# First pair's keys and queries through hardware queues, second batch's loads ahead of the weights, last store in halves

## The chip, the cores and the metric

The kernel runs on one core of a Trainium2 chip. The metric is device time in microseconds (us), the median of several executions. The profile is one execution recorded by the hardware profiler; its span is about 1.8 to 2.1 us shorter than the measured time of the same execution. A run is called slow when it is over 1.5% above the fastest run of the same kernel; such runs are left out of every ratio here.

## The reference

Attention over 8 batches, 12 heads, 448 positions and 64 columns a head, with one added to the softmax's denominator, is followed by a feed-forward layer (768 to 2048 to 768) whose activation is a rational function. Inputs and outputs are float32.

```python
def _attn_ref(q, k, v):
    scores = np.matmul(q, k.transpose(0, 1, 3, 2)) / np.sqrt(q.shape[-1])
    m = np.max(scores, axis=-1, keepdims=True)
    e = np.exp(scores - m)
    return np.matmul(e / (np.sum(e, axis=-1, keepdims=True) + np.exp(-m) + 1e-09), v)
# x = attention output as (B*S, H*D)
# h = x @ w_in                              GEMM1
# g = (a0 + a1 h + a2 h^2 + a3 h^3) / (1 + |b0| |h| + |b1| h^2 + 1e-6)
# out = g @ w_out                           GEMM2
```

## The kernel before

Everything is computed in f16 with f32 accumulation. GpSimd issues all loads but those of two small constants (`abc`, `bbc`), and its loads cast f32 to f16 on the way. Batches 0 and 1 are transposed by TensorE (`tq`, `tk`: nine or eight 112-column blocks of queries, four of keys, for each pair of heads), later batches by the DMA. For a pair of heads come score tiles (`sps`), exponentials on ScalarE (`e`), sums (`den`) and products (`u`) with the values, the scaled result (`xt`) on VectorE, and then GEMM1 (`hp`), the rational function and GEMM2 (`op`).

```python
def load_qk(b, qd, which):              # 4 heads a load, from GpSimd, with the cast
    ...
    nc.gpsimd.dma_start(out=loaded[b, which][...], in_=by_quad(src, b, qd))

def transpose_q(b, p):                  # one pair of heads
    tq = ps.tile([128, 9 * T], F16, tag="gen", bufs=4, name="tq")
    for i, g in enumerate(range(g0, g1)):
        nc.tensor.transpose(tq[:, i * T:(i + 1) * T],
                            loaded[b, "q"][:, g * D:(g + 2) * D], ident[0:T, 0:T])
    # turn(): VectorE copies tq to qT
...
load_qk(0, 0, "k")
load_qk(0, 0, "q")
...
abc = const.tile([128, 4], F32)         # the constants a, on every partition
nc.sync.dma_start(out=abc, in_=moe_a.unsqueeze(0).to_broadcast([128, 4]))
bbc = ...                               # the constants b, likewise; VectorE makes |b| of them
...
def weights(b, h, i):
    e = att.tile([T, 2, S], F16, tag="e", name="e", bufs=12)
    nc.scalar.activation(out=e, in_=sps[0:T, :, 0:S], func=AF.Exp, scale=scale)
...
def outputs(b, tl, nh, eng):
    copied(eng, osb[:, nh * HD:(nh + 1) * HD], ops.pop((b, tl, nh))[:, 0:HD])
    if nh == 1:                         # both halves of the row copied: store them
        ...
        store(b - 1, SM, SR, osb[0:SR])
        store(b, SM, SR, osb[SR:128])
```

The order on TensorE, ScalarE, VectorE and GpSimd is fixed when the kernel is built, by a small planner. Each unit of work has a stream, a key, an estimated duration, the units that it depends on, and the buffers that it takes; the planner takes the unit that can start soonest, then the one with the lowest key. GEMM1 of batch 0 cannot start before all 12 heads of batch 0 are through, so up to there TensorE has only scores, sums, products and transposes. The order of the first loads was

```python
first_loads(("k0", 0), ("q0", 0), ("q0", 1), ("k0", 1), ("v0", 0), ("q0", 2), ("k0", 2),
            ("v0", 1), ("v0", 2), ("q1", 0), ("k1", 0), ("q1", 1), ("w", 0), ("w", 1),
            ("k1", 1), ("w", 2), ("w", 3), ("q1", 2), ("k1", 2), ("v1", 0), ...)
```

The softmax here doesn't subtract the row's maximum and nothing guards it: scores larger than these inputs give would overflow.

Of the kernel before, what the change touches and what calls it, by code (L numbers as in the profile page):

```python
# [16 lines left out]
class Plan:  # L17
# [29 lines left out]
    def order(self, switch, reluctance):  # L47
        at = dict.fromkeys(self.streams, 0)
        mode = None
        while at:  # L50
            ahead = defaultdict(list)
            for s, i in at.items():
                name, key, cost, fn, deps, takes, m = self.streams[s][i]
                r = self.ready(deps, takes)
                if r is None:
                    continue
                for eng in cost:
                    t = max(self.free[eng], r)
                    k = key
                    if eng == "PE" and m != mode:  # L60
                        k += reluctance
                    ahead[eng].append((t, k, s))
            first = None
            for eng, some in ahead.items():
                soon = min(t for t, _, _ in some)
                k, t, s = min((k, t, s) for t, k, s in some if t <= soon + 1e-9)
                if first is None or t < first[0]:
                    first = t, eng, s
# [19 lines left out]
def kernel(  # L88
# [30 lines left out]
    nc.scalar.preload_act_table_set("natural_log_exp_and_others")  # L119
# [12 lines left out]

    loaded = {}
    NB = H * NJ // 2

    def load_qk(b, qd, which):
        w = NJ * D
        if qd == 0:
            if which == "q":
                q4 = ld.tile([T, D + H * NJ * D + D], F16, tag="q4", name="q4")  # L140
                eng = nc.vector if b == 0 else nc.gpsimd
                eng.memset(q4[:, 0:D], 0.0)
                eng.memset(q4[:, D + H * NJ * D:], 0.0)
                loaded[b, "q"] = q4
            else:
                loaded[b, "k"] = ld.tile([T, H * NJ * D], F16, tag="k4", name="k4")
        src, o = (q, D) if which == "q" else (k, 0)
        nc.gpsimd.dma_start(
            out=loaded[b, which][:, o + 4 * qd * w:o + 4 * (qd + 1) * w].rearrange(
                "p (h x) -> p h x", x=w),  # L150
            in_=by_quad(src, b, qd))
# [60 lines left out]
    load_qk(0, 0, "k")  # L212
    load_qk(0, 0, "q")
# [34 lines left out]

    def load_w_out(i):
        if i == 0:  # L250
            nc.gpsimd.tensor_copy(out=gate[0:1, 0:1], in_=loaded[2, "qT"][0:1, 2 * NB * T:2 * NB * T + 1])
# [3 lines left out]

    xts = {}
    ets = {}


    sps_of = {}  # L260

    def scores(b, h, i):
        qT, kT = loaded[b, "qT"], loaded[b, "kT"]
        sps = ps.tile([128, 2, 512], F32, tag="sps", bufs=2, name="sps")
        for half in range(2):
            r = slice(64 * half, 64 * half + 64)
            c = (4 * h + 1 - half) * T
            nc.tensor.matmul(  # L268
                out=sps[0:T, half, 0:S],
                lhsT=kT[r, (2 * h + i) * T:(2 * h + i + 1) * T],  # L270
                rhs=qT[r, c:c + S], start=True, stop=True,
            )
# [8 lines left out]
    def by_heads(dst, b, qd, w):  # L281
        for j in range(NJ):
            for t in range(4):
                nc.tensor.matmul(  # L284
                    out=dst[32 * t:32 * t + 32, 0:S], lhsT=w(4 * qd + t, j),
                    rhs=ets[b, 4 * qd + t, j // 2][:, j % 2, :],
# [7 lines left out]
    def sums(b, qd):  # L294
        dens[b, qd] = ps.tile([128, 512], F32, tag="gen", bufs=4, name="den")
        by_heads(dens[b, qd], b, qd, lambda h, j: ones)

    def sums_ln(b, qd):
        rdens[b, qd] = att.tile([128, S], F32, tag="rden", name="rden")
        nc.scalar.activation(out=rdens[b, qd], in_=dens.pop((b, qd))[:, 0:S],  # L300
                             func=AF.Ln, bias=one_c)

    def sums_inv(b, qd):
        nc.scalar.activation(out=rdens[b, qd], in_=rdens[b, qd], func=AF.Exp, scale=-1.0)

    def products(b, qd, half):
        v4 = loaded[b, "v"]
        u = us[b, qd, half] = ps.tile([128, 512], F32, tag="gen", bufs=4, name="u")
        by_heads(u, b, qd, lambda h, j: v4[:, h, j, 32 * half:32 * half + 32])

    def attended(b, qd, half):
        if (qd, half) == (0, 0):
            xts[b] = xp.tile([128, NDC, S], F16, tag="xt", name="xt")
        nc.vector.tensor_tensor(  # L314
            out=xts[b][:, 2 * qd + half, :], in0=us.pop((b, qd, half))[:, 0:S],
            in1=rdens[b, qd], op=ALU.mult
        )
# [3 lines left out]
    def gemm1(b, fc):  # L321
        xt = xts[b]
        hp = ps.tile([128, 512], F32, tag="gen", bufs=4, name="hp")
        for c in range(NDC):
            nc.tensor.matmul(  # L325
                out=hp[:, 0:S], lhsT=w_in_sb[:, c, fc * 128:(fc + 1) * 128],
                rhs=xt[:, c, :], start=(c == 0), stop=(c == NDC - 1),
            )
        hps[b, fc] = hp
        if fc % FG == 0:  # L330
            gs[b, fc // FG] = gp.tile([128, FG, S], F16, tag="g", name="g")
# [3 lines left out]
    def copied(eng, out, src):  # L335
        if eng == "ACT":
            nc.scalar.activation(out=out, in_=src, func=AF.Copy)
        else:
            nc.vector.tensor_copy(out=out, in_=src)  # L339

    def hidden(b, fc, eng):
        copied(eng, gs[b, fc // FG][:, fc % FG, :], hps.pop((b, fc))[:, 0:S])
# [8 lines left out]
    def temp(tag, f0, n):  # L351
        return moe.tile([128, FG, S], F16, tag=tag, name=tag)[:, f0:f0 + n, :]

    def rational(b, gi, f0, n, step):
        h = gs[b, gi][:, f0:f0 + n, :]
        at = b, gi, f0
        if step == 0:
            m = ns[at] = temp("w", f0, n)
            nc.vector.tensor_scalar(out=m.bitcast(U16), in0=h.bitcast(U16),
                                    scalar1=0x7FFF, scalar2=None, op0=ALU.bitwise_and)  # L360
        elif step == 1:
            c = cs[at] = temp("c", f0, n)
# [31 lines left out]
    def store(b, c0, n, src):  # L394
        dst = out[b * S:(b + 1) * S, :].rearrange("(p j) d -> j p d", j=NJ)
        r = 0
        while r < n:
            j, p0 = divmod(c0 + r, T)
            m = min(T - p0, n - r)
            nc.sync.dma_start(out=dst[j, p0:p0 + m], in_=src[r:r + m, :])  # L400
# [19 lines left out]
    def outputs(b, tl, nh, eng):  # L420
        if nh == 0:
            osbs[b, tl] = moe.tile([128, DM], F32, tag="osb", name="osb")
        osb = osbs[b, tl]
        copied(eng, osb[:, nh * HD:(nh + 1) * HD], ops.pop((b, tl, nh))[:, 0:HD])
        if nh == 1:
            if tl < NW:
                store(b, tl * 128, 128, osb)
            else:
                store(b - 1, SM, SR, osb[0:SR])
                store(b, SM, SR, osb[SR:128])  # L430
# [4 lines left out]
        free=dict(DMA=3.7, PE=3.0, ACT=3.0, DVE=4.0),  # L435
# [4 lines left out]
    def load_step(stream, key, b, qd, which):  # L440
        takes = [(which + "4", (which, b))] if qd == 0 else []
        fn = (lambda: load_v(b, qd)) if which == "v" else (lambda: load_qk(b, qd, which))
        if (b, qd) == (0, 0) and which != "v":
            fn = None
        add(stream, ("ld", which, b, qd), key, {"DMA": (1.2, 4.4)}, fn, takes=takes)
# [11 lines left out]
    def first_loads(*steps):  # L457
        for what, i in steps:
            if what == "w":
                w_in_step(i)  # L460
            else:
                load_step("ld", 0, int(what[1]), i, what[0])

    first_loads(("k0", 0), ("q0", 0), ("q0", 1), ("k0", 1), ("v0", 0), ("q0", 2), ("k0", 2),
                ("v0", 1), ("v0", 2), ("q1", 0), ("k1", 0), ("q1", 1), ("w", 0), ("w", 1),
                ("k1", 1), ("w", 2), ("w", 3), ("q1", 2), ("k1", 2),
                ("v1", 0), ("v1", 1), ("v1", 2))
    for b in range(2, B):
# [6 lines left out]
        if b == 2:  # L475
            for i in range(NWO):
                add("ld", ("w_out", i), 0, {"DMA": (15.7 / NWO, 15.7 / NWO + 3)},
                    lambda i=i: load_w_out(i), deps=[("xb", 2, 2)])

    EV = -100  # L480
    for b in range(B):
        for p in range(NP):
            n = b * NP + p
            if b < 2:
                for which, fn, busy, copy in (("q", transpose_q, 0.7, (0.55, 0.7)),
                                              ("k", transpose_k, 0.3, (0.3, 0.45))):
                    first = [(which + "T", (which + "T", b)) for which in "qk"]
                    add("tp", ("tp", b, p, which), n - 0.6, {"PE": (busy, busy + 0.1)},
                        lambda b=b, p=p, fn=fn: fn(b, p),
                        deps=[("ld", which, b, p // 2)] + (  # L490
                            [("ld", which, b, (p + 1) // 2)]
                            if which == "q" and p < NP - 1 else []),
# [6 lines left out]
            for h in (2 * p, 2 * p + 1):  # L499
                at = n + 0.5 * (h % 2)  # L500
                if b < 2:
                    turned_by = [("tc", b, p, "q"), ("tc", b, p, "k")]
                else:
                    turned_by = [("xb", b, i) for i in range(3)]
                for i in range(2):
                    add("s", ("s", b, h, i), at, {"PE": (0.23, 0.33)},
                        lambda b=b, h=h, i=i: scores(b, h, i), deps=turned_by,
                        takes=[("sps", ("sps", b, h, i))],
                        uses=[("qT", b), ("kT", b)], mode="rows")
                    add("ex", ("ex", b, h, i), at, {"ACT": (0.797, 0.95)},  # L510
                        lambda b=b, h=h, i=i: weights(b, h, i), deps=[("s", b, h, i)],
                        takes=[("e", ("e", b, h, i))], uses=[("sps", b, h, i)])
        for qd in part:
            n = b * NP + 2 * qd
            es = [(b, h, i) for h in range(4 * qd, 4 * qd + 4) for i in range(2)]
            add("av", ("den", b, qd), n + 2.02, {"PE": (0.76, 0.86)},
                lambda b=b, qd=qd: sums(b, qd), deps=[("ex",) + x for x in es],
# [119 lines left out]
```

## Time and profile before

| | before |
|---|---|
| median of 4 runs | 441.56 us (440.56 to 441.81) |
| span of the profiled run (441.07 us) | 439.3 us |
| first transpose | 7.09 us |
| first exponential | 10.18 us |
| first GEMM1 matmul | 38.78 us |
| last matmul ends | 434.19 us |

The page's busy times and the granted clock in 40 slices of 11 us (tenths of full speed). PE stands for TensorE's matmuls, PEld for its weight loads, DVE for VectorE, ACT for ScalarE, POOL for GpSimd, SP for SyncE:

```profile
PE 422.8 (96%) x3346; PEld 214.6 (49%) x3346; DVE 361.9 (82%) x536; ACT 309.0 (70%) x331; POOL 88.3 (20%) x145
...
PEclk9998999999999999999999999999999999999999
```

TensorE is nearly always occupied, but that does not say that it works at full rate. Counting matmuls by kind and pricing each at the shortest duration that the timeline shows for it (GEMM1 unit 1.14 us, GEMM2 unit 2.6, pair of score matmuls 0.23, a unit of sums or products 0.76) gives an estimate of 400.6 us for all of them. The rest is lost mainly at the start. The timeline of TensorE, ScalarE and VectorE there (start us, duration us, engine, line, operation, out<-in, count, and in brackets the idle time before and what ended it):

```profile
7.09 1.00 PE L196 MATMUL tq<-ident,q 112*128 112x112 f16 x9 [7.09 <-DMA q<-in_q_dram]
...
9.51 0.99 PE L268 MATMUL sps<-qT,kT 64*112 64x448 f16 x4
...
10.18 1.72 ACT L278 ACTIVATE e<-sps 112x896 f16<-112x896 f32 x2 [8.16 <-PE sps L268]
...
12.34 2.53 ACT L278 ACTIVATE e<-sps 112x896 f16<-112x896 f32 x3 [0.44 <-PE sps L268]
```

Only 12 us into the run do exponentials follow one another without gaps. The chain that ended last, at the end of the first batch's attention (start us, us, what), and two windows of 1 us in the same stretch (busy us and number of instructions of each engine, granted clock, DMA share, GB/s):

```profile
28.64 4.96 ACT e L278 x6
...
33.65 0.62 PE sps L268 x2
34.27 1.61 PE den L284 x13
35.88 2.05 PE u L284 x25
...
38.94 1.14 PE hp L325 x6
```

```profile
core 0: us, PE busy (x) PEld busy (x) DVE busy (x) ACT busy (x) POOL busy (x), PEclk, DMA share, GB/s
32.00:33.00 1.00, 0.56 (x4) 0.25 (x4) 0.00 (x0) 1.00 (x2) 0.69 (x2) 1.00 1.23 203
34.00:35.00 1.00, 1.00 (x14) 0.39 (x16) 0.00 (x0) 1.00 (x2) 0.60 (x1) 0.50 1.27 198
```

ScalarE's exponentials lead the chain. TensorE does little beside them from 29 us on (0.40 to 0.56 of each microsecond up to 33), the clock falls to half at 33.4 us, and the sums and products of the last four heads take 3.7 us in place of 2.4. The Trainium skill ("TensorE: Matmul & The Clock Gate", "What's actually happening") says that the array's clock is halved after an idle window of about 3.4 us and released after a busy one of that length. This trace agrees in the half rate and in the length: by its clock record (part of the trace, no view of the profile) 0.50 was granted for 3.41 us from 33.42.

### The profile page before, as it was taken

Reading aid. Unit: us, or ns where it says so; the run is one execution under the profiler, and the core shown is the slowest. Engines: PE = TensorE matmul, PEld = TensorE weight load, DVE = VectorE, ACT = ScalarE, POOL = GpSimd, SP = SyncE. Lnnn points to the kernel's source line nnn. Section 1 sums busy time; section 2 is a strip of 40 time slices with the busy share of each in tenths; the row PEclk is TensorE's granted clock in tenths of the full one; section 3 lists DMA queues with packets and bytes.
Section 4 is the critical chain, followed back from the end, with each engine's and each line's share of the span. In section 5 each row is a group of like instructions: output and inputs, shape, how many; then the busy total and the mean of one; then the engine's idle time right before and its main releaser. Section 6 shows DMA issues by size and latency. Waiting matters only on the chain.

```text
span 439.3 us, 8052 instructions
## 1 busy us (share of the span) xinstructions
PE 422.8 (96%) x3346; PEld 214.6 (49%) x3346; DVE 361.9 (82%) x536; ACT 309.0 (70%) x331; POOL 88.3 (20%) x145
## 2 busy tenths in 40 slices
PE   3979999999999999999999999999999999999995
PEld 2534544445444544545445445454544455556663
DVE  2533899999999988799899988799979768999821
ACT  1997998897898785677887856868699674674400
POOL 8466025503241005020050001020000000004100
PEclk9998999999999999999999999999999999999999
DMA  9999989999899169911798049410011011102222
GB/s 123 199 203 197 183 144 184 203 183 198 179 156 181 38 127 154 172 36 38 139 185 131 1 98 170 95 36 17 23 36 36 3 37 36 39 0 73 72 73 72
DMA packets 93476, 46.90 MB, mean 107 GB/s; under 512 B 52480, under 2 KB 89856, under 8 KB 93440
## 3 DMA queue, kind: packets, MB, share of 16 engines
q0 software_dynamic: 38848, 22.81, 38.2%
q1 hardware_dynamic: 54592, 23.58, 27.4%
q8 instruction: 26, 0.43, 0.4%
q14 instruction: 10, 0.08, 0.1%
HBM read 45.62 MB, written 11.01 MB: 129 GB/s over the span
## 4 chain that ended last, share of the span: by engine, by line
PE 83%; DVE 8%; ACT 6%; issue 1%; DMA 1%; POOL 0%; POOLq 0%
PE op L412 34%; PE hp L325 28%; PE sps L268 9%; PE u L284 7%; PE den L284 4%; ACT e L278 4%; DVE g L339 2%; DVE w L372 1%; DMA q<-in_q_dram 1%; DVE w L374 1%; ACT c L379 1%; ACT c L381 1%; DVE g L377 1%; PE tq L196 1%; DVE xt L314 1%
## 5 line engine op out<-in xcount | busy, mean ns | idle before, releaser
L278 ACT ACTIVATE e<-sps 112x896 f16<-112x896 f32 x192 | 165.9, 914 | 57.6 <-PE sps L268 57.0
L325 PE MATMUL hp<-xt,w_in_sb 128*128 128x448 f16 x768 | 158.0, 353 | 0.0
L412 PE MATMUL op<-w_out_sb,g 128*128 128x384 f16 x768 | 131.1, 327 | 0.0
L325 PEld LDWEIGHTS <-w_in_sb 128*128 128x128 f16 x768 | 70.2, 98 | 76.4 <-issue 17.3
L412 PEld LDWEIGHTS <-g 128*128 128x128 f16 x768 | 73.5, 98 | 53.8 <-issue 5.4
L379 ACT ACTIVATE c<-c,oneeps_c 128x1792 f16<-128x1792 f16 (+1 forms) x33 | 57.4, 1743 | 29.9 <-DVE c L367 29.9
L339 DVE CAST g<-hp 128x448 f16<-128x448 f32 x109 | 66.8, 617 | 13.3 <-PE hp L325 13.3
L372 DVE TENSOR_TENSOR w<-w,g 128x1792 f16<-128x1792 f16 (+1 forms) x66 | 70.0, 1061 | 0.7
L391 POOL COPY gx<-g 128x256 f16<-128x256 f16 x32 | 19.9, 641 | 237.9 <-DVE g L377 136.1
L268 PE MATMUL sps<-qT,kT 64*112 64x448 f16 x384 | 61.9, 380 | 4.3 <-ACT e L278 3.9
L381 ACT ACTIVATE c<-c 128x1792 f16<-128x1792 f16 (+1 forms) x33 | 54.2, 1647 | 0.3
L314 DVE TENSOR_TENSOR xt<-u,rden 128x448 f16<-128x448 f32 x48 | 27.8, 616 | 21.6 <-PE sps L268 8.1
L339 DVE COPY osb<-op 128x384 f32<-128x384 f32 x51 | 28.2, 553 | 20.6 <-PE op L412 20.6
L374 DVE TENSOR_SCALAR w<-w,abc 128x1792 f16<-128x1792 f16 (+1 forms) x66 | 44.3, 672 | 0.6
L284 PE MATMUL u<-e,v 112*32 112x448 f16 x768 | 41.1, 356 | 0.0
L268 PEld LDWEIGHTS <-kT 64*112 64x112 f16 x384 | 20.1, 126 | 41.6 <-issue 40.2
L377 DVE TENSOR_TENSOR g<-w,c 128x1792 f16<-128x1792 f16 (+1 forms) x33 | 35.0, 1061 | 1.0
L367 DVE TENSOR_TENSOR c<-c,w 128x1792 f16<-128x1792 f16 (+1 forms) x33 | 35.0, 1062 | 0.8
L156 POOL DMA_DIRECT2D v<-in_v_dram x24 | 17.7, 740 | 70.0 <-PE u L284 67.8
L284 PEld LDWEIGHTS <-v 112*32 112x32 f16 x768 | 20.8, 98 | 16.4 <-issue 1.0
L369 DVE TENSOR_SCALAR w<-g,abc 128x1792 f16<-128x1792 f16 (+1 forms) x33 | 24.2, 733 | 0.6
L363 DVE TENSOR_SCALAR c<-w,babs 128x1792 f16<-128x1792 f16 (+1 forms) x33 | 24.3, 738 | 0.3
(36 smaller groups left out, 217.7 us busy)
## 6 DMA issues: line engine op xcount, KB each, us to landing
k<-in_k_dram POOLq DMA_DIRECT2D x24, 224.0 KB, 9.9
q<-in_q_dram POOLq DMA_DIRECT2D x24, 224.0 KB, 9.3
v<-in_v_dram POOLq DMA_DIRECT2D x24, 224.0 KB, 8.6
w_in_sb<-in_moe_w_in_dram POOLq DMA_DIRECT2D x16, 192.0 KB, 7.9
w_out_sb<-in_moe_w_out_dram POOLq DMA_DIRECT2D x4, 768.0 KB, 11.7
out_dram<-osb SPq DMA_DIRECT2D x8, 336.0 KB, 2.7
out_dram<-osb SPq DMA_DIRECT2D x8, 288.0 KB, 3.0
out_dram<-osb SPq DMA_DIRECT2D x8, 240.0 KB, 2.6
```

The source lines that it names most:

```text
L268: nc.tensor.matmul(out=sps[0:T, half, 0:S], lhsT=kT[r, (2 * h + i) * T:(2 * h + i + 1) * T], rhs=qT[r, c:c + S], start=True, stop=True,)
L278: nc.scalar.activation(out=e, in_=sps[0:T, :, 0:S], func=AF.Exp, scale=scale)
L284: nc.tensor.matmul(out=dst[32 * t:32 * t + 32, 0:S], lhsT=w(4 * qd + t, j), rhs=ets[b, 4 * qd + t, j // 2][:, j % 2, :], start=(j == 0), s ...
L325: nc.tensor.matmul(out=hp[:, 0:S], lhsT=w_in_sb[:, c, fc * 128:(fc + 1) * 128], rhs=xt[:, c, :], start=(c == 0), stop=(c == NDC - 1),)
L339: nc.vector.tensor_copy(out=out, in_=src)
L367: nc.vector.tensor_tensor(out=c, in0=c, in1=m, op=ALU.mult)
L372: nc.vector.tensor_tensor(out=m, in0=m, in1=h, op=ALU.mult)
L374: nc.vector.tensor_scalar(out=m, in0=m, scalar1=a1 if step == 5 else a0, scalar2=None, op0=ALU.add)
L377: nc.vector.tensor_tensor(out=h, in0=m, in1=c, op=ALU.mult)
L379: nc.scalar.activation(out=c, in_=c, func=AF.Ln, bias=oneeps_c)
L381: nc.scalar.activation(out=c, in_=c, func=AF.Exp, scale=-1.0)
L412: nc.tensor.matmul(out=op[:, 0:HD], lhsT=lhs(fc), rhs=w_out_sb[:, fc, nh * HD:(nh + 1) * HD], start=(fc == 0), stop=(fc == NFC - 1),)
```

## The change

The intent is to start the first exponential sooner, to have more work for TensorE before the first GEMM1, and to shorten the end. The first two key heads and three query heads are loaded as f32 through the hardware queues of ScalarE and SyncE and narrowed by VectorE and ScalarE, because, as the Trainium skill says ("DMA: Bandwidth & Descriptors", "SWDGE vs HWDGE vs iDMA"), a cast during the load is possible from GpSimd only. Loads that GpSimd issues are called software loads below. The second batch's keys and queries are loaded ahead of the first weight. The last output tile is stored in halves by two queues. The planner got new keys, and until 35 us of its own reckoning it changes between kinds of matmul without reluctance.

```diff
+    early = {"k": 2, "q": 3}
+    def load_early(which):
+        ...
+        wide[which] = moe.tile([128, DM], F32, tag="osb", name="osb")
+        eng = nc.sync if which == "q" else nc.scalar
+        eng.dma_start(out=wide[which][0:T, 0:n * w]..., in_=by_quad(...)[:, 0:n])
+    def narrow(which, eng):             # k on VectorE, q on ScalarE
+        copied(eng, loaded[0, which][:, o:o + n], wide[which][0:T, 0:n])
-    load_qk(0, 0, "k")
-    load_qk(0, 0, "q")
+    load_early("k")
+    nc.scalar.preload_act_table_set("natural_log_exp_and_others")
+    load_early("q")
+    load_qk(0, 0, "k", early["k"])      # the heads that are left, as before
+    load_qk(0, 0, "q", early["q"])
 ...
-    first_loads(("k0", 0), ("q0", 0), ("q0", 1), ("k0", 1), ("v0", 0), ("q0", 2), ("k0", 2),
-                ("v0", 1), ("v0", 2), ("q1", 0), ("k1", 0), ("q1", 1), ("w", 0), ("w", 1), ...
+    first_loads(k0.0, q0.0, q0.1, q0.2, k0.1, v0.0, k0.2, v0.1, k1.0, q1.0, k1.1, k1.2,
+                q1.1, q1.2, v0.2, w.0, w.1, w.2, v1.0, k2.0, v1.1, w.3, ...)   # shortened
 ...
+        if (b, tl, nh) == (B - 1, NW, 1):
+            for half, to in enumerate((nc.sync, nc.scalar)):
+                r = slice(64 * half, 64 * half + 64)
+                copied(("DVE", "ACT")[half], osb[r, HD:], ops[b, tl, nh][r, 0:HD])
+                store(b - 1 + half, SM, SR, osb[r], HD, DM, to)
 ...  (new keys S_AT, G1_AT, G2_AT, R_AT, LN_AT; patience and calm in the planner;
 ...   branches for split query halves and for reciprocals on VectorE, never taken)
```

The counts of matmuls (3346) and of changes between full, row-tiled and column-tiled matmuls (220) stay the same in the instruction order.

## The prediction

> **What bounds the kernel now.** The page shows TensorE busy 96% of 439.3 us. Priced at undisturbed durations from the timeline (GEMM1 unit 1.14, GEMM2 unit 2.6, score pair 0.23, sums or products unit 0.76 us), all matmuls make 400.6 us. The other 38.7 us, from counting matmuls per stretch:
> - 7.1 us before the first matmul: in the waits, the first transpose waits for the first query load, issued by GpSimd at 2.09.
> - About 10 us up to the first GEMM1 at 38.9. Until then only 21.5 us of matmul work was done: attention of batch 0 is limited by ScalarE (26 exponentials of 0.83 us, three Ln/Exp pairs of 1.2 us), with too little other work. At 34 to 36 us the granted clock is 0.50, and sums plus products take 3.7 us, not 2.4. The Trainium skill ("TensorE: Matmul & The Clock Gate", "What's actually happening") has the clock halve when TensorE was little busy; the trace agrees.
> - About 16 us from 38.9 to 434.2: 189 changes between full, row and column tiling at about 0.07 us (from 140 to 380 us, 8.0 us lost over 114 changes), so 13 us, and some 3 us of waits, mostly while VectorE is full (50 to 140 us).
> - 5.1 us after the last matmul: copy 0.56, two store issues, landing 2.5.
>
> **What the change does.** Matmuls stay 3346; the instruction order shows tiling changes stay 220. The branches for split query halves and VectorE reciprocals are never taken.
> 1. Start. Two key heads and three query heads come as f32 through hardware queues, then one copy each (estimate 0.55 us VectorE, 0.7 us ScalarE). The skill ("DMA: Bandwidth & Descriptors", "SWDGE vs HWDGE vs iDMA") allows casts on the software path only, hence the copies. Issued at 0.7 and 1.2 us; small hardware loads here land in 2.9 us, 336 KB stores in 2.7, so I estimate queries landed near 5.0 and the first transpose at 5.8, not 7.1. Scores follow the first transposed pair, not the second: first exponential near 8.6, not 10.2.
> 2. More filler. With batch 1's loads ahead of the weights, all twelve of its transposes and more scores precede GEMM1: 24.0 us of work instead of 21.5. Spread between the scores, they should remove the clock dip (1.3 us). One more exponential precedes the last inverse (0.8 us). First GEMM1 near 37.5 us.
> 3. Weights land 3 to 4 us later, still before 37.5; the last quarter is not needed until about 50.
> 4. VectorE gets the same work, 2 to 3 us earlier; the order delays its demand around 140 us, so its limit there should relax.
> 5. Tail: last copy split over two engines, 96 KB stores on two queues, neither issue waiting for the other: 0.6 us.
>
> **Sum.** 37.5 + 376.6 of work + 13.0 for 185 changes + 2 of waits = 429.1, tail 4.5: span 433.6. Measured time is 2 us above the span: about 435.8 us, 5.6 us or 1.3% faster. All of it is on the chain that ends last, since TensorE is full from GEMM1 on.
>
> Predicted 435.8 us, range 433.2 to 439.0. Faster by over 2%: 0.10; within 2%: 0.89; slower: 0.01.
>
> **What would show it.** First matmul at 5.5 to 6.2; first exponential at 8.2 to 9.2; no clock dip near 34 us; first GEMM1 at 37 to 38.3; TensorE end near 429; tail 4.5.
>
> **What would make it wrong.** Hardware loads slowed by the software loads beside them (first transpose at 7); a transpose of batch 1 waiting for its load; late weights; VectorE saturated earlier, so that waits grow between 60 and 140 us and eat the lead.

## The result

| | before | after | predicted after |
|---|---|---|---|
| median | 441.56 us | 438.46 us (437.78 to 439.23, 4 runs) | 435.8 us |
| ratio | | 0.9935, interval 0.9912 to 0.9957 | 0.987 |
| span of the profiled run (441.07, 437.78 us) | 439.3 us | 436.0 us | 433.6 us |
| first transpose | 7.09 us | 7.12 us | 5.8 us |
| first exponential | 10.18 us | 9.87 us | 8.6 us |
| first GEMM1 matmul | 38.78 us | 38.98 us | 37.5 us |
| last matmul ends | 434.19 us | 431.64 us | 429.1 us |
| from there to the end | 5.11 us | 4.36 us | 4.5 us |

A ratio is the mean time of one kernel's fast runs over that of the other's of the same rounds, so it is not quite the ratio of the medians; the intervals are of 95%. The change gains 3.1 us of the predicted 5.6. Its profile is of its fastest execution, 0.7 us below its median.

The page after, the same two rows:

```profile
PE 420.3 (96%) x3346; PEld 213.5 (49%) x3346; DVE 361.3 (83%) x536; ACT 308.4 (71%) x334; POOL 91.1 (21%) x145
...
PEclk9999999999999999999999999999999999999999
```

The clock row no longer has the 8 in the fourth slice. The start, in the timeline:

```profile
1.22 0.46 SPq L170 DMA_DIRECT2D osb<-in_q_dram  x1
...
5.16 0.43 DVE L137 CAST k<-osb 112x512 f16<-112x512 f32 x1 [4.15 <-DMA osb<-in_k_dram]
...
6.22 0.84 ACT L135 ACTIVATE q<-osb 112x768 f16<-112x768 f32 x1 [3.75 <-DMA osb<-in_q_dram]
...
7.12 1.02 PE L221 MATMUL tq<-ident,q 112*128 112x112 f16 x9 [7.12 <-DVE babs L255]
...
9.87 1.72 ACT L318 ACTIVATE e<-sps 112x896 f16<-112x896 f32 x2 [2.81 <-PE sps L308]
...
11.23 0.95 PE L221 MATMUL tq<-ident,q 112*128 112x112 f16 x8
...
12.77 1.72 ACT L318 ACTIVATE e<-sps 112x896 f16<-112x896 f32 x2 [1.17 <-PE sps L308]
```

The keys are narrowed from 5.16 and the queries from 6.22, 5.0 us after their issue at 1.22. The first transpose starts when ScalarE is done with the narrowing, at the same time as before. The wait is entered under a small VectorE operation on a constant (`babs`), which ended at the same moment; the narrowing ended at 7.06. Then the third exponential comes only at 12.77, 0.43 us later than before, with 1.17 us of idle ScalarE ahead of it. The landings, from the list of DMA issues of the first 8 us (out<-in, queue, KB each, us from issue to landing):

```profile
osb<-in_q_dram SPq DMA_DIRECT2D x1, 336.0 KB, 5.0
osb<-in_k_dram ACTq DMA_DIRECT2D x1, 224.0 KB, 4.4
...
abc<-in_moe_a_dram SPq DMA_DIRECT2D x1, 2.0 KB, 4.2
```

The end of the first batch's attention in the chain, which answers to the one shown of before:

```profile
34.09 0.40 PE sps L308 x2
34.48 0.87 PE den L330 x16
35.36 0.33 PE sps L308 x2
35.68 1.63 PE u L330 x32
...
39.04 1.05 PE hp L387 x5
```

Sums and products take 0.87 and, with a pair of scores between, about 1.6 us: full rate. The end of the run, in both kernels:

```profile
428.83 5.36 PE L412 MATMUL op<-w_out_sb,gx 128*128 128x384 f16 x32
...
434.23 0.56 DVE L339 COPY osb<-op 128x384 f32<-128x384 f32 x1 [2.04 <-PE op L412]
```

```profile
426.28 5.36 PE L474 MATMUL op<-w_out_sb,gx 128*128 128x384 f16 x32
...
431.69 0.55 DVE L137 COPY osb<-op 64x384 f32<-64x384 f32 x1 [2.04 <-PE op L474]
432.32 0.48 ACT L135 ACTIVATE osb<-op 64x384 f32<-64x384 f32 x1 [20.94 <-DMA out_dram<-osb]
```

Split at the first GEMM1, the profiled spans are 38.78 + 400.5 us before and 38.98 + 397.0 us after. So the start brought nothing; the 3.3 us of the spans come from the part after it: 2.75 us up to the last matmul, 0.75 us behind it, less the 0.2 by which GEMM1 starts later.

### The profile page after: what moved, and what is told of

Read it like the earlier page. It is cut to its first block, busy times and chain, and to the rows that moved or that the text cites. A ratio compares the mean times of both kernels' runs of the same rounds, so it can differ in the third digit from the quotient of the medians.

```text
span 436.0 us, 8073 instructions
## 1 busy us (share of the span) xinstructions
PE 420.3 (96%) x3346; PEld 213.5 (49%) x3346; DVE 361.3 (83%) x536; ACT 308.4 (71%) x334; POOL 91.1 (21%) x145
## 3 DMA queue, kind: packets, MB, share of 16 engines
q0 software_dynamic: 38288, 22.53, 37.5%
## 4 chain that ended last, share of the span: by engine, by line
PE 91%; ACT 5%; DMA 2%; DVE 0%; SPq 0%; issue 0%
PE hp L387 34%; PE op L474 33%; PE sps L308 11%; PE u L330 8%; PE den L330 5%; ACT e L318 4%; DMA bbc<-in_moe_b_dram 1%; PE tq L221 1%; DMA out_dram<-osb 0%; ACT c L441 0%; DVE qT L235 0%; DVE osb L137 0%; ACT rden L349 0%; SPq L462 0%; ACT osb L135 0%
## 5 line engine op out<-in xcount | busy, mean ns | idle before, releaser
L453 POOL COPY gx<-g 128x256 f16<-128x256 f16 x32 | 22.7, 727 | 241.3 <-DVE g L439 131.3
L308 PE MATMUL sps<-qT,kT 64*112 64x448 f16 x384 | 61.0, 377 | 4.2 <-ACT e L318 3.3
L137 DVE COPY osb<-op 128x384 f32<-128x384 f32 (+1 forms) x51 | 28.1, 552 | 21.1 <-PE op L474 21.1
```

What stands on the lines that cost most here:

```text
L137: nc.vector.tensor_copy(out=out, in_=src)
L308: nc.tensor.matmul(out=sps[0:T, half, n * w:(n + 1) * w], lhsT=kT[r, (2 * h + pair) * T:(2 * h + pair + 1) * T], rhs=qT[r, c:c + w], start ...
```

## The experiments

Two questions: why did the early loads bring nothing, and where do the 2.75 us come from? All twelve kernels gave correct results. "Before" is the kernel before on the same chip in the same rounds. The medians are over all runs, the ratios over fast ones; the one slow run of a variant is 450.1 us, of tail_only. The changed kernel itself was timed only in its own rounds, so that differences between it and a variant go through the kernel before or through profiles.

| run | median, us | before, us | ratio (interval) | first transpose | first exponential | first GEMM1 | span | span less first GEMM1 |
|---|---|---|---|---|---|---|---|---|
| the change | 438.46 | 441.56 | 0.9935 (0.9912 to 0.9957) | 7.12 | 9.87 | 38.98 | 436.0 | 397.0 |
| soft_start | 438.71 | 441.75 | 0.9925 (0.9895 to 0.9954) | 7.29 | 10.02 | 40.06 | 437.2 | 397.1 |
| tail_only | 442.0 | 441.75 | 1.0005 (0.9966 to 1.0045) | 7.36 | 10.44 | 39.34 | 439.0 | 399.7 |
| q_queue_alone | 437.15 | 441.75 | 0.9894 (0.9861 to 0.9927) | 6.40 | 9.15 | 38.20 | 435.2 | 397.0 |
| soft_held | 442.27 (one run) | 441.75 | none | 6.93 | 9.69 | 43.10 | 440.2 | 397.1 |
| warm | 436.77 | 441.56 | 0.9893 (0.988 to 0.9906) | 7.15 | 9.28 | 37.31 | 434.5 | 397.2 |
| split_queues | 436.89 | 441.56 | 0.9899 (0.9885 to 0.9912) | 5.21 | 9.12 | 38.49 | 435.5 | 397.0 |
| split_warm | 436.02 | 441.56 | 0.9879 (0.9866 to 0.9892) | 5.47 | 8.89 | 37.27 | 434.4 | 397.1 |
| mid_warm | 440.81 | 441.56 | 0.9997 (0.9972 to 1.0022) | 7.03 | 10.57 | 40.17 | 440.7 | 400.5 |
| late_filler | 442.81 | 442.0 | 1.0026 (1.0013 to 1.0039) | 7.12 | 9.88 | 40.84 | 441.0 | 400.2 |
| old_loads | 443.03 | 442.0 | 1.0026 (1.0013 to 1.0039) | 7.73 | 10.48 | 41.64 | 441.5 | 399.9 |
| split_warm_late | 435.88 | 442.0 | 0.987 (0.9854 to 0.9887) | 5.30 | 7.43 | 36.71 | 433.8 | 397.1 |
| mid_warm2 | 441.77 | 442.0 | 1.0016 (0.9982 to 1.0049) | 7.02 | 10.11 | 37.94 | 443.4 | 405.5 |

The last column is the key to the table: in every variant that keeps the change's order of work (with all twelve transposes of batch 1 ahead of GEMM1) it is 397.0 to 397.2 us, whatever happens at the start. What the start gains or loses until the first GEMM1 goes one to one into the profiled span. But each row's profile is of one execution, and by the clock records of the traces full rate is first granted at 12.58 us in the change, 15.97 in soft_start, 11.72 in q_queue_alone, 12.91 in split_queues and 6.07 in warm: some of the differences between first GEMM1s come from that moment.

### soft_start: the change without its early loads

```diff
-    load_early("k")
+    new_qk(0, "k")
+    new_qk(0, "q")
     nc.scalar.preload_act_table_set("natural_log_exp_and_others")
-    load_early("q")
-    load_qk(0, 0, "k", early["k"])
-    load_qk(0, 0, "q", early["q"])
+    load_qk(0, 0, "k")
+    load_qk(0, 0, "q")
     # and narrow() does nothing
```

> The changed kernel with the first keys and queries loaded as before, by GpSimd with the cast in the load, and no copies; the TensorE order is untouched. Theory 1 (the early loads brought nothing, because the first transpose came at 7.12 with them and at 7.09 without): first transpose near 7.1, time within 0.5 us of the changed kernel, 438.0 to 439.0. Theory 2 (the early loads brought about 1.3 us that another delay, such as the new order at the start, hides): first transpose at 8 or later, time 439.5 or more.

Measured: 438.71 us, first transpose at 7.29. The early loads are worth nothing that these runs can resolve, as theory 1 said. Its profiled run has GEMM1 1.1 us later than the change's, because TensorE ran at half rate until 15.97 us there and until 12.58 in the change, by the clock records; the times of the two kernels still agree within 0.3 us of median.

### q_queue_alone and soft_held: why the queries landed late

```diff
 # q_queue_alone
-    nc.sync.dma_start(out=abc, in_=moe_a...)
+    nc.scalar.dma_start(out=abc, in_=moe_a...)
-    nc.sync.dma_start(out=bbc, in_=moe_b...)
+    nc.scalar.dma_start(out=bbc, in_=moe_b...)
 # soft_held
+    for which, c in (("k", 2 * NJ * D), ("q", D + 3 * NJ * D), ...):
+        nc.gpsimd.tensor_copy(out=loaded[0, which][0:1, c:c + 1], in_=wide["q"][0:1, 0:1])
     load_qk(0, 0, "k", early["k"])      # now wait for the query load through those bytes
```

> The changed kernel with the two broadcast constants moved to ScalarE's queue, behind the keys and the table load, so that the query load is first on its own queue. Theory A (the query load is late because its queue first passes the 128 pieces of 16 bytes of a constant, and because a queue passes its 1 KB pieces slowly): queries land near 5.1 instead of 6.2, first transpose near 6.1, first exponential near 8.9, time 437.0 to 437.8. Theory B (software loads beside them take the DMA engines): landing and time as in the changed kernel.

> The changed kernel with all software loads held back until the query load has landed; slower on purpose, one look at when the hardware loads land. Theory B (contention with the software loads): keys land by 4.0 and queries by 5.0. Theory A (the hardware queues' own pace): keys still land at 4.6 to 5.2 and queries at 5.8 to 6.3.

In soft_held the first packets of a software load start at 8.2 us, after both landings. The timeline of the narrowing:

```profile
5.04 0.43 DVE L137 CAST k<-osb 112x512 f16<-112x512 f32 x1 [4.04 <-DMA osb<-in_k_dram]
6.04 0.84 ACT L135 ACTIVATE q<-osb 112x768 f16<-112x768 f32 x1 [3.55 <-DMA osb<-in_q_dram]
```

Keys and queries land at 5.04 and 6.04, inside theory A's ranges, against 5.16 and 6.22 in the change. So without any software load the queries still land a microsecond after the forecast 5.0. That does not make contention, which the prediction had named as its first danger, worth only 0.2 us, because the two runs differ in one thing more: by the packet records SyncE's queue started first in soft_held (first packets at 1.76 us, ScalarE's at 2.38), and ScalarE's did in the change (1.81, SyncE's at 2.35). Of the runs with the change's load commands on both queues and software loads beside them, one, old_loads, has the order of soft_held (1.78 and 2.36):

```profile
5.65 0.55 DVE L137 CAST k<-osb 112x512 f16<-112x512 f32 x1 [4.64 <-DMA osb<-in_k_dram]
...
6.83 0.84 ACT L135 ACTIVATE q<-osb 112x768 f16<-112x768 f32 x1 [4.34 <-DMA osb<-in_q_dram]
```

Against that run, soft_held's landings are 0.61 and 0.79 us sooner. About 0.5 us of this is there before the first software packet, at 4.40: the last piece of the constant starts at 4.20, in soft_held at 3.70. With one profile each, what the software loads cost the landing stays open, between 0.2 and 0.8 us. With the queries alone on their queue:

```profile
5.50 0.84 ACT L135 ACTIVATE q<-osb 112x768 f16<-112x768 f32 x1 [3.01 <-DMA osb<-in_q_dram]
...
6.40 1.02 PE L221 MATMUL tq<-ident,q 112*128 112x112 f16 x9 [6.40 <-ACT q L135]
```

They are issued at 0.75 instead of 1.22 and land 0.72 us sooner; about 0.47 us of that is the earlier issue; the rest we put down to the pieces of the constant that are no longer ahead, which no run separates. The time falls to 437.15 us, inside the expectation (437.0 to 437.8), but the landing at 5.5 is later than the 5.1 expected. Counting the records of DMA packets of the change's profiled run by queue shows the pace:

```
packets started in each half us (16 B = the constant's, 1 KB = keys or queries)
from, us   ScalarE's queue (keys)   SyncE's queue                  software
1.5        15 of 1 KB               -                              -
2.0        66                       12 of 16 B                     -
2.5        55                       45, nearly all 16 B            -
3.0        39                       63, mixed                      -
3.5        28                       66, mixed                      -
4.0        37, last small ones      134 of mostly 1 KB             2
4.5        -                        139                            44
5.0        -                        95, last small ones            120
```

Half of the 1 KB pieces take 46 ns or less on their engine, and there are 16 engines, so they are far from full up to 4 us. The windows view of the change says the same (DMA share and GB/s are the last two columns; the share, which can exceed 1, stays near 1.45 from 9 us on):

```profile
2.00:3.00 1.00, 0.00 (x0) 0.00 (x0) 0.00 (x0) 0.47 (x1) 1.00 (x4) 1.00 0.46 125
3.00:4.00 1.00, 0.00 (x0) 0.00 (x0) 0.00 (x0) 0.00 (x0) 0.92 (x3) 1.00 0.67 134
9.00:10.00 1.00, 0.79 (x4) 0.26 (x4) 0.15 (x1) 0.13 (x1) 1.00 (x2) 1.00 1.45 196
```

### split_queues: the queries on both hardware queues

```diff
+        some = [(nc.sync, 0, 2), (nc.scalar, 2, 3)] if which == "q" else [(nc.scalar, 0, n)]
+        for eng, h0, h1 in some:
+            eng.dma_start(...)          # heads h0 to h1; queries are issued ahead of the keys
     # and the constants on ScalarE's queue, as in q_queue_alone
```

> Two query heads alone on the SyncE queue, the third query head and then the keys on ScalarE's, the two constants behind them. Theory A (each hardware queue passes its 1 KB pieces at its own pace): queries, 224 pieces deep on each queue at most, land near 4.8 instead of 5.5 with the queries alone on their queue, first transpose near 5.7, time about 436.4. Rival (a common pace for both queues together, about 200 pieces a us): queries land no earlier than 5.3, time as with the queries alone, 437.1.

```profile
4.31 0.84 ACT L135 ACTIVATE q<-osb 112x768 f16<-112x768 f32 x1 [1.34 <-DMA osb<-in_q_dram]
...
5.21 1.02 PE L222 MATMUL tq<-ident,q 112*128 112x112 f16 x9 [5.21 <-ACT q L135]
...
6.73 0.59 DVE L253 TENSOR_SCALAR babs<-bbc 128x2 f32<-128x2 f32 x1 [1.24 <-DMA bbc<-in_moe_b_dram]
...
7.43 0.67 DVE L236 COPY qT<-tq 128x1008 f16<-128x1008 f16 x1
```

The queries land at 4.31, sooner than theory A had it, and the first transpose is at 5.21. But the first exponential comes at 9.12, where it was with the queries alone on their queue: the copy of the transposed queries (`qT<-tq`) stands on VectorE behind `babs`, which waits until 6.73 for the constants, now last in their queue. The time is 436.89 us, not 436.4. An operation of 0.17 us in the change, harmless as long as the queries were not much sooner than it, has become the wait.

### warm: matmuls on zeros while TensorE waits

```diff
+    still = const.tile([128, 128], F16)
+    nc.vector.memset(still, 0.0)
+    idle = ps.tile([128, 2, 512], F32, tag="sps", bufs=2, name="idle")
+    for i in range(56):
+        nc.tensor.matmul(out=idle[:, 0, 0:128], lhsT=still, rhs=still, start=True, stop=True)
```

> The changed kernel with 56 matmuls on zeros, read by nobody, on TensorE while it waits for the first queries; nothing else. Theory C (the new order of the first pairs loses time because TensorE still runs at half rate: 112-column transposes take 113 ns each up to 12.5 us and half that later, so that ScalarE sits 1.2 us idle before its third exponential): transposes at full rate from the start, first exponential near 9.0 instead of 9.9, third near 11.0 instead of 12.8, first GEMM1 near 37.4, time 436.5 to 437.3. Rival (ScalarE's gap comes from loads or copies, not from the rate): third exponential later than 12.3, time 438.0 to 438.8.

```profile
7.15 0.62 PE L221 MATMUL tq<-ident,q 112*128 112x112 f16 x9 [0.39 <-ACT q L135]
...
9.28 5.16 ACT L324 ACTIVATE e<-sps 112x896 f16<-112x896 f32 x6 [2.18 <-PE sps L314]
```

The nine transposes take 0.62 us, not 1.02, and six exponentials follow one another from 9.28. GEMM1 starts at 37.31, 1.67 us sooner than with the change, and the time is 436.77 us. Theory C holds. The change's order is the one that needs this: it issues scores after the first transposed pair and then puts the transposes of the next two pairs before the next scores, at half rate. So ScalarE, served sooner once, then idles.

### split_warm and split_warm_late: both, and the constants out of the way

split_warm joins the edits of split_queues and warm (with 44 matmuls on zeros). split_warm_late also moves the two VectorE operations of `babs` to their first use:

```diff
-    nc.vector.tensor_scalar(out=babs, in0=bbc, scalar1=-1.0, ...)     # at the start
-    nc.vector.tensor_tensor(out=babs, in0=babs, in1=bbc, op=ALU.max)
 def rational(b, z, gi, f0, n, step):
+        if step == 0 and not ns:        # at the first group
+            (the same two operations)
```

> Both: queries on two queues and 44 matmuls on zeros ahead. If both causes are separate they add: first exponential near 7.8, third near 9.9, first GEMM1 near 36.3, time 435.3 to 436.0, which is what the prediction had put on record for the change. If another limit stands behind them (loads of the next pairs), the third exponential stays above 10.8 and the time above 436.3.

> Queries on two queues, matmuls on zeros ahead, and the two small VectorE operations on a constant moved from the start to their first use, since with the queries landed at 4.4 the copy of the first transposed queries stood behind them until 7.4. First exponential near 7.2 instead of 8.9. If loads of the next pairs don't hold it: first GEMM1 near 35.8, time 434.6 to 435.4. If they do: third exponential later than 10.3, time near 436.0 as without the move.

split_warm gave 436.02 us, at the edge of its expectation (435.3 to 436.0), with `babs` in the way as in split_queues. In its profile the two repairs did not add: the first exponential came at 8.89 where 7.8 was expected, and GEMM1 at 37.27 (36.3 expected), no sooner than with warm alone (37.31). For split_warm_late:

```profile
7.43 3.53 ACT L321 ACTIVATE e<-sps 112x896 f16<-112x896 f32 x4 [2.18 <-PE sps L311]
...
10.66 0.37 PE L230 MATMUL tk<-ident,k 112*128 112x112 f16 x4 [1.06 <-DMA k<-in_k_dram]
...
11.99 2.67 ACT L321 ACTIVATE e<-sps 112x896 f16<-112x896 f32 x3 [1.03 <-PE sps L311]
```

The first exponential comes at 7.43, 2.4 us sooner than with the change, but then TensorE's transposes of the third pair's keys wait 1.06 us for a software load of keys, and ScalarE idles 1.03 us until 11.99. GEMM1 starts at 36.71 where 35.8 was hoped for, and the time is 435.88 us, above the expected 434.6 to 435.4. Against split_warm the move shows in the profile (433.8 against 434.4), not beyond doubt in the times. It is the fastest kernel; the ratio to the kernel before is 0.987 where the change has 0.9935, in rounds on different chips or at different times.

### late_filler and old_loads: where the 2.75 us come from

late_filler leaves the loads alone and holds the transposes of pairs 3 to 5 of batch 1 back:

```diff
                         deps=[("narrow", which)] * (b == 0 and p < 2)
+                        + [("g1", 0, 0, 2 * p - 5)] * (b == 1 and p > 2)
```

old_loads puts the loads in the order of the kernel before and lets the planner follow; transposes then wait for their later loads, and go behind GEMM1 units in the order.

> The changed kernel, loads untouched, with the transposes of pairs 3 to 5 of the second batch held behind GEMM1 units of the first in the instruction order; the first GEMM1 then follows 21.5 us of matmul work as in the kernel before, instead of 24.0. Theory (the gain is the 2.5 us of work moved into time in which TensorE would have idled): time 440.4 to 441.5, 2 to 2.5 us above the changed kernel, first GEMM1 not earlier than 38.5. Rival (the gain comes from the start, the loads or the tail, and TensorE has slack later): within 0.7 us of the changed kernel.

> The changed kernel with the loads in the order of the kernel before (weights between the second batch's loads); the schedule follows, and puts 22.0 us of work before the first GEMM1 instead of 24.0. Theory (the load order matters since it lets all transposes come early): time 1.5 to 2.5 us above the changed kernel, 440.0 to 441.0. Rival (the load order is worth nothing): within 0.5 us of 438.5.

late_filler runs as the change up to 28.7 us (from 15 us on its matmuls start within 0.03 us of the change's). Then:

```profile
32.00:33.00 1.00, 0.48 (x4) 0.13 (x2) 0.00 (x0) 1.00 (x2) 0.57 (x1) 1.00 1.26 204
34.00:35.00 1.00, 0.89 (x6) 0.30 (x9) 0.00 (x0) 1.00 (x3) 0.54 (x1) 0.50 1.45 197
```

```profile
34.66 1.69 PE L330 MATMUL den<-e,ones 112*32 112x448 f16 x16
...
37.20 3.18 PE L330 MATMUL u<-e,v 112*32 112x448 f16 x32
...
40.84 2.44 PE L387 MATMUL hp<-xt,w_in_sb 128*128 128x448 f16 x12
```

TensorE is 0.48 busy in the microsecond from 32 (0.81 in the change), the clock falls to half for 6.83 us from 33.55 (clock record), sums take 1.69 us and products 3.18, and GEMM1 starts at 40.84, 1.9 us later than with the change; the rest of the run is 3.2 us longer, of which the transposes moved there take 2.8. Together the profiled spans differ by 5.0 us (441.0 against 436.0). The expectation of 440.4 to 441.5 us was too small, because it counted the 2.5 us of moved work and left out the clock: 442.81 us. old_loads gave 443.03 us, also more than expected (440.0 to 441.0), with the same dip in its clock (6.83 us from 33.49). About 0.6 us of its profile's loss lies at the start and need not come from the load order: its hardware loads landed late, as shown above, and its first transpose came at 7.73. So the early transposes are the change's gain, by two ways: they use time in which TensorE idled, and they keep its clock up. They are possible because the second batch's loads come before the weights. Without them, the new order is slower than the kernel before: the ratio is 1.0026 in both runs, with an interval clear of 1.

### tail_only: the last store in halves on the kernel before

The edit is the `outputs` and `store` part of the diff above.

> The kernel before with the last store in halves and nothing else. If the tail gives what the traces showed (from the last matmul to the end 5.1 us before, 4.4 after), the time falls by 0.5 to 0.9 us, to about 440.8. Rival: the 3.1 us of the whole come from work before GEMM1 alone, and the tail is worth under 0.2 us.

Measured 442.0 us (441.65 without the slow run) against 441.75 (interval of the ratio 0.9966 to 1.0045): the times do not resolve half a microsecond. In its profile the last matmul ends at 434.52 and the span at 439.0, so 4.5 us lie behind it, where the kernel before has 5.11 and the change 4.36. The gain of the tail is therefore read from three profiles, not from times.

### mid_warm and mid_warm2: the clock dip alone, on the kernel before

```diff
         sps_of[b, h, i] = sps       # in scores(); mid_warm2, mid_warm had 12 row-tiled ones
+        for n in range(8 if (b, h) in [(0, x) for x in range(8, H)] + [(1, 0)] else 0):
+            nc.tensor.matmul(out=sps[:, n % 2, S:512], lhsT=ident, rhs=ident[:, 0:64],
+                             start=True, stop=True)     # columns that nobody reads
```

> The kernel before with 12 small matmuls, read by nobody, behind each score tile of heads 8 to 11 of the first batch, so that TensorE is busier there. Theory (the clock dip of 33 to 37 us in the kernel before is due to little TensorE work and costs 1.3 us, which the changed kernel gets back by putting transposes there): no dip in the clock, sums and products there in 2.4 us, first GEMM1 near 37.6, time lower by 1.0 to 1.5 us, 440.0 to 440.8. Rival (the dip costs nothing, since ScalarE bounds this stretch): same time within 0.4 us.

> The kernel before with 8 matmuls over all 128 rows, read by nobody, behind each score tile of heads 8 to 11 of the first batch and head 0 of the second, which keeps TensorE busy through the stretch in which the clock dipped (the lighter try did not prevent the dip). Theory: no dip, sums and products there in 2.4 us instead of 3.7, time lower by 0.7 to 1.3 us. Rival (the dip costs nothing): same within 0.4 us of the kernel before.

Both are inconclusive as times. In mid_warm the dip only moved to 35 us in the profiled run. By the mean clocks listed with the runs it was absent in the other five of the six (0.997 to 1.0; the dip of 3.41 us leaves 0.996): four of these took 440.4 to 440.9 us, where the fast runs of the kernel before in the same rounds took 440.9 to 441.9, and the fifth 443.85. That hints at a cost below a microsecond and does not show it. In mid_warm2 it was gone and GEMM1 started at 37.94, 0.84 us sooner than before:

```profile
34.00:35.00 1.00, 1.00 (x18) 0.60 (x21) 0.00 (x0) 1.00 (x2) 0.57 (x1) 1.00 1.28 197
```

but two of its six runs took about 445 us, the profiled one among them (443.4 us of span). There, TensorE waited 3.4 us near 112 us, ahead of scores of batch 3. The profile enters the wait under ScalarE; we read it as a wait for a DMA transpose of the queries, which took 11.09 us from 102.25 where it took 8.30 us from 100.99 in the kernel before. No run tests that. The other four runs took 440.7 to 442.4 us. What the dip alone costs the kernel before is thus not settled; that it costs the changed order about 1.9 us of its start when it comes back, twice as long, is shown by late_filler.

## Why the prediction was wrong

The direction, and the class (within 2%), were right; 438.46 us lies in the range of 433.2 to 439.0, but the gain is 3.1 us where 5.6 were forecast.

- **Step 1, "Start", is the step that failed.** It had the queries land near 5.0 and the first transpose at 5.8; they landed at 6.22, 5.0 us after their issue, and it came at 7.12, no sooner than before. The term of 1.3 us in it was in fact 0. The estimate took landing times of small loads and of stores, and did not ask what else stood in the same queue or how fast a queue passes 336 pieces. The runs showed that both matter: alone in its queue the load lands at 5.50 (q_queue_alone), on two queues at 4.31 (split_queues). The danger that the prediction named, software loads beside them, is not enough to explain it: without them the queries still land at 6.04 (soft_held). What part they have stays open (0.2 to 0.8 us, from single profiles).
- **The same step also left out the half rate at the start.** "Scores follow the first transposed pair, not the second: first exponential near 8.6" was to be pure gain. With transposes at 113 ns each, the next pair came late, ScalarE idled 1.17 us, and the third exponential was 0.43 us later than before. With a warm TensorE the gap is gone (warm, 1.7 us sooner at GEMM1). The prediction spoke of the clock gate at 34 us and did not apply it to the first microseconds.
- **Step 2, "More filler", was right.** 24.0 us of work before GEMM1, no dip in the clock, and the rest of the run shorter by 3.5 us with the tail. late_filler and old_loads lose all of it. That GEMM1 would start at 37.5 fell with step 1: 38.98, which is 1.5 us later.
- **The waits behind GEMM1** were put at 2 us. From the first GEMM1 to the end the prediction had 396.1 us (433.6 less 37.5); every profiled run with this order has 397.0 to 397.2. This term was 0.9 us too small. The estimated costs of a tiling change (0.07 us) and of the waits were not separated by any run.
- **Step 3** held: no wait for a weight shows in the waits of TensorE. **Step 4** cannot be told apart from that 0.9 us. **Step 5** held in the profiles: 4.36 us where 4.5 was forecast.

The span was missed by 2.4 us: 1.5 from the start and 0.9 from behind GEMM1. With the start repaired (split_warm_late) GEMM1 came at 36.71 and the median was 435.88 us, which is where the prediction had put the change. That the figures meet is partly luck: GEMM1 came 0.8 us sooner than the forecast 37.5, and the part after it took 1.0 us longer than the forecast 396.1.

What stays open: how much of the late landing is due to the small pieces of the constant, to the order in which the two queues start, and to the software loads; what the clock dip costs the kernel before by itself; and which waits make the 0.9 us.

## What to carry to other kernels

When a load is put on a hardware queue to arrive sooner, look at what is already in that queue, at how many pieces it has, and at the first operation of each in-order engine that stands between its landing and its use; a tiny constant can become the wait. Fill the time before TensorE's main work with transposes or other work that has to be done anyway, because it saves its own length and can keep the clock up as well. And split a run at the point where its bottleneck takes over: when all variants with one order of work have the same time from there to the end, as here 397 us, everything else is decided ahead of that point.

## What the Trainium skill lacked or had wrong

- "DMA: Bandwidth & Descriptors" ("Issuing engines are not separate DMA queues") says that issuing from several engines saves only the sequencer's time, usually small. Here moving one of three query heads to the second hardware queue, ahead of the keys, brought the landing from 5.50 to 4.31 us (4.58 and 4.40 in split_warm and split_warm_late), though the query loads were issued at 0.75 us in both cases. With the queries on one queue the DMA engines were not full meanwhile (share 0.56, 1.08 and 1.02 in the microseconds from 2 to 5, against 1.45 later).
- The same page ("Anatomy of one DMA — SWDGE (gpsimd) path") fits about 2.0 us plus bytes over 436 GB/s for the software path. No page gives a counterpart for hardware queues with many small pieces; the estimate by that fit for 344 KB (336 pieces of 1 KB) is 2.8 us, and the run shows 5.0 us behind a constant and 4.7 us alone in the queue.
- "TensorE: Matmul & The Clock Gate" has the cold start, and its advice for modelling is that the ramp costs under 1% of a typical span. Here it decided a comparison of that size: GEMM1 started at 38.98 us without and at 37.31 with matmuls on zeros ahead, and the medians, from different rounds, are 438.46 and 436.77 us, 0.4% apart. The clock row of the profile does not show it: it reads 9 from the start, while transposes took 113 ns instead of 69 and the trace's clock record grants full rate from 12.58 us only.
- The same page says that a busy window releases the clock and an idle one halves it. Here it was halved without idle windows: in the kernel before with TensorE 0.40 to 0.56 busy from 29 to 33 us, and in mid_warm, at 34.9, with it 0.79 to 0.88 busy from 30 to 34 (64-column, row-tiled matmuls among its work) and 0.45 from 34 to 35. Apart from a remark on transposes, no page says how the kind of matmul counts, nor how busy a window must be to keep the clock.
